# Gradient kernel of an attention layer on one core: o/dQ products of two units together in even units, dK products in odd units

## The chip, the core and the metric

The kernel runs on one core of one Trainium2 chip. The metric is the device time in microseconds (us) of that core; several executions are timed, and a comparison uses executions of both kernels on the same chip. Engines: PE is TensorE (PEld its weight loads), ACT is ScalarE, DVE is VectorE, POOL is GpSimd, SP the engine that issues most DMAs.

## The reference, cut to what matters

The reference computes a linear-attention block (A) and a softmax attention block with 16 query heads and one key/value head (B), and all their gradients. Nearly all the time is in block B, with S = 2048 tokens, 16 heads of 28 channels:

```python
scores = jnp.einsum("bhqd,bkd->bhqk", q, k) * (Dh ** -0.5)
p = _softmax(scores, axis=-1)
o = jnp.einsum("bhqk,bkd->bhqd", p, v)
return (lambda x, *d: x.transpose(*d))(o, 0, 2, 1, 3).reshape(B, S, H * Dh) @ wo
# ... and jax.vjp of all of it with grad_out
```

## The kernel before

The main loop has 512 units. Unit u handles 256 queries, 2 heads and 256 keys; eight units make a block (b = u // 8), after which an accumulator is complete. The forward part of unit u runs beside the backward part of unit w = u - 16. Each unit does, in the program's order:

- "scores": on PE, q.k products into `sps` (two 128x512 tiles, of three buffers) and dO.v products into `dps` (two tiles, of two buffers), contraction over 32 rows: shape 32*128;
- ACT: exp of the first `sps` half (L710), copy of the second `dps` half to `cp` (L717), exp of the second `sps` half (L720);
- DVE: first half of `dsT` = dps times eT (L715); POOL: second half of `dsT` = cp times eT (L718); later DVE transposes dsT into `dsx` (L853);
- PE: dK products (shape 32*32), o, dQ and dV products (shape 128*32).

```python
def mmt(out, lhsT, rhs, pos, start, stop):                       # all these matmuls have line L591
    nc.tensor.matmul(out, lhsT=lhsT, rhs=rhs, start=start, stop=stop, tile_position=pos, ...)

for u in range(NU + 28):                                         # NU = 512
    w = u - 16
    ...
    rows_SD(u, sp, dp)                                           # scores: 4 + 4 matmuls of 256 columns
    ACT:  et[u % 2, 0] = exp(sp[0])                              # L710
    DVE:  dst[0] = dp[0] * ew[0]                                 # L715, dsT of unit w
    ACT:  cp = copy(dp[1])                                       # L717
    POOL: dst[1] = cp * ew[1]                                    # L718
    ACT:  et[u % 2, 1] = exp(sp[1])                              # L720
    ...                                                          # u % 8 == 1: identF transposes of oTs, then rl, onat, don
    ...                                                          # u % 8 == 2: prod; 4: Dq; 6: identB transposes of don -> doT
    x = u - 28                                                   # dK: 3, 3, 3, 3, 2, 2 groups of four matmuls in 6 units of 8
    ...
    v, y = u - 1, u - 18
    for t2 in range(2):                                          # o of unit v, dQ of unit y: 8 matmuls
        ...oq[32*h...]      += vaug . eT[v]
        ...oq[64 + 32*h...] += kn . dsT[y]
    ...                                                          # dV: 8 matmuls of 512 columns in u % 8 == 2 and 3
    ...                                                          # 14 blocks: output projection in a unit u % 8 == 0
    if v % 8 == 7: DVE: oTs = oq[0:64]                           # L844
    if y % 8 == 7: ACT: qT_B = oq[64:128] * scale                # L847, the "dQ copy"
    DVE: dsx[b] = transpose(dsT[y])                              # L853
```

(The block above is abridged and partly paraphrased.)

Of the kernel before, what the change touches and what calls it, by code (L numbers as in the profile page):

```python
# [24 lines left out]
def kernel(  # L25
# [540 lines left out]
    NB = 64  # L566
    NU = NB * 8
# [3 lines left out]
    with ExitStack() as cs_:  # L571
# [16 lines left out]
        eT, eN, dsT, dsx, qX, onat, don, doT, rl, oTs, prod = ({} for _ in range(11))  # L588

        def mmt(out, lhsT, rhs, pos, start, stop):  # L590
            nc.tensor.matmul(out, lhsT=lhsT, rhs=rhs, start=start, stop=stop, tile_position=pos,  # L591
                             skip_group_check=True)

        def blk(b):
            qc, pair = divmod(b, 8)
            return qc, pair, pair // 2, pair % 2
# [91 lines left out]
        with tc.manual_schedule():  # L688
            for u in range(NU + 28):
# [37 lines left out]
                if e >= 0 and e % 8 == 0 and e // 8 < NB:  # L727
                    b = e // 8
# [24 lines left out]
                if e >= 0 and e % 8 == 0 and e // 8 < NB:  # L753
                    b = e // 8
# [9 lines left out]
                if e >= 0 and e % 8 == 0 and e // 8 < NB:  # L764
                    b = e // 8
# [4 lines left out]
                if e >= 0 and e % 8 == 0 and e // 8 < NB:  # L770
                    b = e // 8
# [7 lines left out]
                    doT[b] = pw_.tile([P, 256], BF16, name="doT")  # L779
                    nc.vector.tensor_copy(out=doT[b][r:r + 64, :], in_=tp2[r:r + 64, 0:256])  # L780

                x = u - 28
                if 0 <= x and x // 8 < NB and x % 8 < 6:
                    b = x // 8
                    qc, pair, g, hp = blk(b)
                    m0 = 3 * (x % 8) - max(0, x % 8 - 4)
                    for m in range(m0, m0 + (3 if x % 8 < 4 else 2)):
                        h, B, s = m // 8, (m // 2) % 4, m % 2
                        for a in range(4):
                            rhs = dsx[b][32 * a:32 * a + 32, :, h, :, :].rearrange(  # L790
                                "p u t (b i s) -> p u t b i s", b=4, s=2)[:, :, :, B, :, s]
                            mmt(dk_acc[32 * a:32 * a + 32, :],
                                qX[qc][32 * a:32 * a + 32, B, s, pair * 64 + 32 * h:pair * 64 + 32 * h + 32],
                                rhs, (32 * a, 32 * a), b == 0 and m == 0, b == NB - 1 and m == 15)

                v = u - 1
                y = u - 18
                for t2 in range(2):
                    if 0 <= v < NU:
                        b, tp = divmod(v, 8)  # L800
                        t = 2 * tp + t2
                        for h in range(2):
                            mmt(oq[32 * h:32 * h + 32, 0:256], vaug[:, t, :],
                                eT[v // 2][:, v % 2, h, t2 * 256:(t2 + 1) * 256], (0, 32 * h), t == 0, t == 15)
                    if 0 <= y < NU:
                        b, tp = divmod(y, 8)
                        t = 2 * tp + t2
                        for h in range(2):
                            mmt(oq[64 + 32 * h:96 + 32 * h, 0:256], kn[:, t, :],
                                dsT[y][:, h, t2 * 256:(t2 + 1) * 256], (0, 64 + 32 * h), t == 0, t == 15)  # L810
                if u >= 18 and u % 8 in (2, 3) and (u - 18) // 8 < NB:
                    b, h = divmod(u - 18, 8)
                    for qb in range(2):
                        for c in range(4):
                            rhs = eN[4 * b + c][:, :, :].rearrange("p (u h t q) k -> p u h t q k", u=2, h=2,
                                                                   t=2)[:, :, h, :, qb, :]
                            mmt(dv_acc[32 * c:32 * c + 32, :], don[b][:, qb, h, :], rhs, (0, 32 * c),
                                b == 0 and h + qb == 0, b == NB - 1 and h + qb == 2)
# [20 lines left out]
                if u % 64 in (16, 24) and u > 64:  # L839
                    out_proj(2 * (u // 64 - 1) + u % 64 // 8 - 2)  # L840

                if 0 <= v < NU and v % 8 == 7:
                    oTs[v // 8] = pm_.tile([64, 256], F32, name="oTs")
                    nc.vector.tensor_copy(out=oTs[v // 8][:, :], in_=oq[0:64, 0:256])  # L844
                if 0 <= y < NU and y % 8 == 7:
                    qc, pair, g, hp = blk(y // 8)
                    nc.scalar.activation(out=qT_B[g][64 * hp:64 * hp + 64, qc * 256:(qc + 1) * 256],  # L847
                                         in_=oq[64:128, 0:256], func=ACT.Copy, scale=scale)
                if 0 <= y < NU:
                    b, tp = divmod(y, 8)  # L850
                    if tp == 0:
                        dsx[b] = px_.tile([P, 8, 2, 2, 256], BF16, name="dsx")
                    nc.vector.transpose(  # L853
                        out=dsx[b][:, tp, :, :, :].rearrange("p h t c -> p (h t c)").bitcast(F32),
                        in_=dsT[y][:, :, :].rearrange("p h c -> p (h c)").bitcast(F32))
# [82 lines left out]
```

## Time and profile before

| | before |
|---|---|
| median | 1178.23 us of the first 3 runs; 1176.08 us of 4, with the result |
| length of a usual block of eight units | 12.78 us |
| length of the 14 blocks with an output projection | 13.75 us |

The block lengths, here and below, are worked out from the trace: the distance between the ends of ACT's `cp` (L717) eight units apart; "usual" is the length that most blocks without an output projection share. Pairs of units are measured likewise.

From the page of the kernel before: the span, the busy time of the engines, and costly groups (busy us, mean ns of one | idle time of the engine before them and what ended most of it).

```profile
span 1172.0 us, 38434 instructions
PE 1099.7 (94%) x15388; PEld 444.6 (38%) x15388; DVE 885.5 (76%) x1669; ACT 900.9 (77%) x1788; POOL 699.4 (60%) x835
L718 POOL TENSOR_TENSOR dsT<-cp,eT 128x512 bf16<-128x512 bf16 x512 | 590.3, 1153 | 193.2 <-ACT cp L717 156.2
L710 ACT ACTIVATE eT<-sps 128x512 bf16<-128x512 f32 x512 | 307.3, 600 | 42.2 <-PE dps L591 28.3
L717 ACT ACTIVATE cp<-dps 128x512 bf16<-128x512 f32 x512 | 305.1, 596 | 12.0 <-PE dps L591 11.1
L591 PE MATMUL oq<-dsT,R_65 128*32 128x256 bf16 x2048 | 203.1, 278 | 1.1 <-POOL dsT L718 0.9
```

ACT's three instructions take about 0.60 us each but start 0.48 to 0.49 us apart: 1.46 us a unit. ACT hardly idles. The dQ products do not wait for POOL (0.9 us in all). The waits between 300 and 1100 us say the same (total us, times, longest us):

```profile
ACT eT L710 <- PE dps L591: 24.6, 76, 2.9
ACT R_63 L847 <- PE oq L591: 5.2, 14, 0.4
PE oq L591 <- POOL dsT L718: 0.9, 1, 0.9
```

The timeline of the kernel before (start us, us, instruction):

```profile
603.86 0.28 PE L591 MATMUL sps<-R_63,R_65 32*128 32x256 bf16 x2
604.15 0.83 PE L591 MATMUL dk_acc<-dsx,qX 32*32 32x512 bf16 x12
604.66 0.60 ACT L717 ACTIVATE cp<-dps 128x512 bf16<-128x512 f32 x1
604.91 0.29 PE L591 MATMUL oq<-eT,R_65 128*32 128x256 bf16 x2
605.03 0.28 PE L591 MATMUL oq<-dsT,R_65 128*32 128x256 bf16 x2
605.24 0.28 PE L591 MATMUL sps<-R_63,R_65 32*128 32x256 bf16 x2
605.34 1.15 POOL L718 TENSOR_TENSOR dsT<-cp,eT 128x512 bf16<-128x512 bf16 x1
```

Two things are to be seen. Within a shape the groups of four matmuls start 0.11 us (256 columns) or 0.21 us (512) apart, but a change of shape takes longer: oq at 605.03 to sps at 605.24 is 0.21 us. And the dsT of this unit is finished by POOL at 606.49, 1.25 us after the scores of the next unit have started.

### The profile page before, as it was taken

To read this page: it belongs to the slowest core of one execution; us is meant where nothing else is said; L and a number is where in the kernel's file an instruction comes from. 1 tells how busy PE (TensorE), PEld (TensorE's weight loads), DVE (VectorE), ACT (ScalarE), POOL (GpSimd) and SP (SyncE) were. 2 spreads that over 40 slices of the span, in tenths; PEclk is the share of its full clock that TensorE was granted. 3 is DMA by queue.
4 is the path that set the end of the run, shared out by engine and by line. 5 is a ranking of instruction groups with operands and counts; after the bars stand their busy time and mean duration, and the time that the engine had idled before them with its cause. 6 is when DMAs were issued, how large, how long until landed. Compare 5 with 4: busy or idle time off the path is not lost. (4 is left out here: it accounts for less than half of the span.)

```text
span 1172.0 us, 38434 instructions
## 1 busy us (share of the span) xinstructions
PE 1099.7 (94%) x15388; PEld 444.6 (38%) x15388; DVE 885.5 (76%) x1669; ACT 900.9 (77%) x1788; POOL 699.4 (60%) x835
## 2 busy tenths in 40 slices
PE   7999997988989999999999999999999999999998
PEld 4555543333333333333333333333333333333344
DVE  7886400336889898888889888988999899888922
ACT  3453112357989999999999999999999999999511
POOL 9000150003777777777778777877787778777900
PEclk9999998989999999999999999999999999999999
DMA  9779897059999999999999999999999999999962
GB/s 259 126 130 184 160 188 177 20 125 198 180 179 190 188 164 187 190 184 175 189 188 160 199 188 186 162 198 188 152 195 182 189 170 199 184 168 163 240 147 75
DMA packets 684435, 202.91 MB, mean 173 GB/s; under 512 B 651232, under 2 KB 679392, under 8 KB 684256
## 3 DMA queue, kind: packets, MB, share of 16 engines
q1 hardware_dynamic: 673664, 190.26, 94.8%
q10 hardware_dynamic: 9312, 6.65, 2.1%
q0 software_dynamic: 1280, 3.55, 1.1%
q8 instruction: 120, 1.97, 0.7%
q14 instruction: 59, 0.48, 0.1%
HBM read 22.83 MB, written 15.03 MB: 32 GB/s over the span
## 5 line engine op out<-in xcount | busy, mean ns | idle before, releaser
L718 POOL TENSOR_TENSOR dsT<-cp,eT 128x512 bf16<-128x512 bf16 x512 | 590.3, 1153 | 193.2 <-ACT cp L717 156.2
L715 DVE TENSOR_TENSOR dsT<-dps,eT 128x512 bf16<-128x512 f32 x512 | 347.8, 679 | 58.3 <-PE dps L591 37.6
L853 DVE STREAM_TRANSPOSE dsx<-dsT 128x512 f32<-128x512 f32 x512 | 357.8, 699 | 1.3 <-POOL dsT L718 0.3
L710 ACT ACTIVATE eT<-sps 128x512 bf16<-128x512 f32 x512 | 307.3, 600 | 42.2 <-PE dps L591 28.3
L591 PEld LDWEIGHTS <-R_65 32*128 32x128 bf16 (+1 forms) x8192 | 171.5, 92 | 403.3 <-issue 356.1
L717 ACT ACTIVATE cp<-dps 128x512 bf16<-128x512 f32 x512 | 305.1, 596 | 12.0 <-PE dps L591 11.1
L720 ACT ACTIVATE eT<-sps 128x512 bf16<-128x512 f32 x512 | 311.6, 609 | 0.0
L591 PE MATMUL dk_acc<-dsx,qX 32*32 32x512 bf16 x4096 | 290.4, 377 | 0.0
L591 PE MATMUL dps<-doT,R_65 32*128 32x256 bf16 x2048 | 253.9, 271 | 7.7 <-DVE R_64 L824 1.1
L591 PE MATMUL sps<-R_63,R_65 32*128 32x256 bf16 x2048 | 242.9, 276 | 5.9 <-ACT eT L710 2.0
L591 PE MATMUL oq<-eT,R_65 128*32 128x256 bf16 x2048 | 213.8, 278 | 2.5 <-issue 0.3
L591 PE MATMUL oq<-dsT,R_65 128*32 128x256 bf16 x2048 | 203.1, 278 | 1.1 <-POOL dsT L718 0.9
L591 PEld LDWEIGHTS <-qX 32*32 32x32 bf16 x4096 | 69.4, 89 | 94.1 <-issue 54.1
L591 PE MATMUL dv_acc<-eN,don 128*32 128x512 bf16 x1024 | 86.9, 382 | 2.5 <-DMA eN<-eT 2.5
L521 DVE TENSOR_TENSOR osb<-R_65 32x512 bf16<-32x512 bf16 x4 | 1.7, 413 | 74.2 <-ACT R_65 L518 74.2
L380 POOL MEMSET ga<- 64x448 bf16 x2 | 0.9, 468 | 90.8 <-PE agen L337 71.3
L553 POOL MEMSET R_65<- 128x16 bf16 x1 | 0.2, 172 | 70.8 <-DVE R_65 L552 70.8
L748 POOL TENSOR_TENSOR don<-R_64,rl 128x128 bf16<-128x128 bf16 x64 | 25.8, 403 | 21.4 <-DVE rl L740 21.4
L844 DVE COPY oTs<-oq 64x256 f32<-64x256 f32 x64 | 26.5, 414 | 15.1 <-PE oq L591 14.4
L731 PE MATMUL sps<-identF,oTs 64*128 64x64 f32 x128 | 21.3, 247 | 17.0 <-DVE oTs L844 10.6
L591 PEld LDWEIGHTS <-don 128*32 128x32 bf16 x1024 | 34.7, 97 | 4.0 <-issue 3.9
L79 PEld LDWEIGHTS <-R_64 128*128 128x128 bf16 x256 | 23.9, 100 | 28.0 <-issue 10.3
(216 smaller groups left out, 961.2 us busy)
## 6 DMA issues: line engine op xcount, KB each, us to landing
qX<-qn_d SPq DMA_DIRECT2D x128, 64.0 KB
out_dram<-osb ACTq DMA_DIRECT2D x44, 112.0 KB
eN<-eT SPq DMA_TRANSPOSE x256
qn_d<-dsx SPq DMA_DIRECT2D x1, 2048.0 KB
on_d<-onat SPq DMA_DIRECT2D x8, 256.0 KB
xa<-in_A_x_dram SPq DMA_DIRECT2D x8, 224.0 KB
ga<-in_grad_out_dram SPq DMA_DIRECT2D x4, 448.0 KB
xa<-in_grad_out_dram POOLq DMA_DIRECT2D x4, 448.0 KB, 4.7
```

Source lines behind the costliest of these rows:

```text
L79: nc.tensor.matmul(out_ap, lhsT=lhsT, rhs=rhs, start=start, stop=stop, tile_position=(0, 0))
L521: nc.vector.tensor_tensor(out=sq[0:32, :], in0=kT[0:32, qc * 512:(qc + 1) * 512], in1=kT[0:32, qc * 512:(qc + 1) * 512], op=ALU.mult)
L591: nc.tensor.matmul(out, lhsT=lhsT, rhs=rhs, start=start, stop=stop, tile_position=pos, skip_group_check=True)
L710: nc.scalar.activation(out=et[:, u % 2, 0, :], in_=sp[0][:, :], func=ACT.Exp, scale=scale)
L715: nc.vector.tensor_tensor(out=dst[:, 0, :], in0=dp[0][:, :], in1=ew[:, w % 2, 0, :], op=ALU.mult)
L717: nc.scalar.activation(out=cp[:, :], in_=dp[1][:, :], func=ACT.Copy)
L718: nc.gpsimd.tensor_tensor(out=dst[:, 1, :], in0=cp[:, :], in1=ew[:, w % 2, 1, :], op=ALU.mult)
L720: nc.scalar.activation(out=et[:, u % 2, 1, :], in_=sp[1][:, :], func=ACT.Exp, scale=scale)
L731: nc.tensor.transpose(onp[:, qb, :, :].rearrange("p h c -> p (h c)"), oTs[b][0:64, qb * P:(qb + 1) * P], identF[0:64, 0:64], tile_position ...
L748: nc.gpsimd.tensor_tensor(out=dn[:], in0=dnv, in1=r_[:].to_broadcast([P, 2, 2, 32]), op=ALU.mult)
L844: nc.vector.tensor_copy(out=oTs[v // 8][:, :], in_=oq[0:64, 0:256])
L853: nc.vector.transpose(out=dsx[b][:, tp, :, :, :].rearrange("p h t c -> p (h t c)").bitcast(F32), in_=dsT[y][:, :, :].rearrange("p h c -> p ...
```

## The change

The intent is fewer changes of tile shape on PE: scores then dK in odd units, scores then o/dQ/dV of two units in even ones, 16 changes a block instead of 22. No work is added or removed.

```diff
-                x = u - 28
-                if 0 <= x and x // 8 < NB and x % 8 < 6:
+                x = u - 27
+                if 0 <= x and x // 8 < NB and x % 2 == 0:
                     b = x // 8
-                    m0 = 3 * (x % 8) - max(0, x % 8 - 4)
-                    for m in range(m0, m0 + (3 if x % 8 < 4 else 2)):
+                    for m in range(4 * (x % 8 // 2), 4 * (x % 8 // 2) + 4):
 ...
-                v = u - 1
-                y = u - 18
-                for t2 in range(2):
+                v, y = u - 1, u - 17
+                for d in range(4 if u % 2 == 0 else 0):
+                    t2 = d % 2
+                    v_, y_ = v - 1 + d // 2, y - 1 + d // 2
 ...   (o of units v_, dQ of units y_: eT[v_], dsT[y_])
-                if u >= 18 and u % 8 in (2, 3) and (u - 18) // 8 < NB:
+                if u >= 18 and u % 8 in (2, 4) and (u - 18) // 8 < NB:
 ...
-                if 0 <= v < NU and v % 8 == 7:
+                if u % 2 == 0 and 0 <= v < NU and v % 8 == 7:
 ...   (oTs copy on DVE)
-                if 0 <= y < NU and y % 8 == 7:
+                if u % 2 == 0 and 0 <= y < NU and y % 8 == 7:
 ...   (dQ copy on ACT; y is now u - 17, so this falls in the unit of the oTs copy)
+                y = u - 18
```

More of the change, by code (lines that the diff above doesn't have):

```diff
@@ L794 @@
                                 rhs, (32 * a, 32 * a), b == 0 and m == 0, b == NB - 1 and m == 15)
-                v = u - 1
-                y = u - 18
-                for t2 in range(2):
-                    if 0 <= v < NU:
-                        b, tp = divmod(v, 8)
-                        t = 2 * tp + t2
+                v, y = u - 1, u - 17
+                for d in range(4 if u % 2 == 0 else 0):
+                    t2 = d % 2
+                    v_, y_ = v - 1 + d // 2, y - 1 + d // 2
+                    if 0 <= v_ < NU:
+                        t = 2 * (v_ % 8) + t2
                         for h in range(2):
                             mmt(oq[32 * h:32 * h + 32, 0:256], vaug[:, t, :],
-                                eT[v // 2][:, v % 2, h, t2 * 256:(t2 + 1) * 256], (0, 32 * h), t == 0, t == 15)
-                    if 0 <= y < NU:
-                        b, tp = divmod(y, 8)
-                        t = 2 * tp + t2
+                                eT[v_ // 2][:, v_ % 2, h, t2 * 256:(t2 + 1) * 256], (0, 32 * h), t == 0, t == 15)
+                    if 0 <= y_ < NU:
+                        t = 2 * (y_ % 8) + t2
                         for h in range(2):
                             mmt(oq[64 + 32 * h:96 + 32 * h, 0:256], kn[:, t, :],
-                                dsT[y][:, h, t2 * 256:(t2 + 1) * 256], (0, 64 + 32 * h), t == 0, t == 15)
-                if u >= 18 and u % 8 in (2, 3) and (u - 18) // 8 < NB:
-                    b, h = divmod(u - 18, 8)
+                                dsT[y_][:, h, t2 * 256:(t2 + 1) * 256], (0, 64 + 32 * h), t == 0, t == 15)
+                if u >= 18 and u % 8 in (2, 4) and (u - 18) // 8 < NB:
+                    b, h = (u - 18) // 8, (u - 18) % 8 // 2
                     for qb in range(2):
```

## The prediction

> **What bounds it now.** The 512 main units run from about 248 to 1114 us. In the windows view (300 to 1100 us) TensorE is busy about 95%, ScalarE about 95%, VectorE 89%, GpSimd 77%. The timeline shows a repeating block of eight units of 12.78 us (13.75 where the output projection falls in; 14 of 64 blocks). ScalarE's three 512-column instructions of a unit start 0.49, 0.48 and 0.49 us apart when nothing delays them: 1.46 us a unit, and with the dQ copy about 12.05 us a block. So ScalarE is nearly the floor; the other 0.7 us are waits for late scores (waits view: ScalarE eT and cp on dps, 29 us between 300 and 1100). TensorE's score products stretch from 0.13 to 0.47 us in the units where it is ahead, because they need the dP buffer that cp frees.
>
> **What the change does.** It removes changes of tile shape on TensorE: 22 a block become 16. In the timeline, last start to first start is 195 ns from scores to the next shape (about 110 within a shape), 301 from dK to o/dQ (213 within), 205 from o/dQ to scores: 90 to 100 ns a change. The Trainium skill, "TensorEngine Tiling (Array Packing)", Overview, Key Properties, says a mode change drains TensorE; the trace agrees, with these 90 to 100 ns. Saved: about 0.6 us of TensorE a block, 11.1 to 10.5 us. No work is added.
>
> The danger: in even units dQ now reads the dsT of the unit just before (lag 17 instead of 18). Its second half is made by GpSimd in 1.15 us, starting 0.08 us after cp ends. In the trace GpSimd's product of an odd unit ends 0.9 to 1.5 us after the next unit's score products start; the new dQ matmuls want it about 0.55 us after. TensorE is in order ("TensorE: Matmul & The Clock Gate", Part 3: matmuls are strict FIFO), so dV and the next scores wait behind it.
>
> That makes a loop over two units, from the end of cp(odd) to the end of the next cp(odd): GpSimd 1.23, semaphore 0.06, last dQ round 0.11, change to scores 0.21, scores to first exp 0.42, exp to cp 0.49, cp 0.60: 3.12 us, against ScalarE's 2.92 for two units. Where dV follows in the even unit (two pairs of four), 0.43 more: 3.54. In the pair with the dQ copy ScalarE sets about 3.33. Sum 3.33 + 3.54 + 3.54 + 3.12 = 13.53 us a block, +0.75 against 12.78, times 64 = +48 us. The blocks with an output projection win back about 0.3 us each, 4 to 5 us; start and end nearly unchanged.
>
> **Predicted: 1219 us**, range 1194 to 1240. Faster by over 2%: 0.09; within 2%: 0.17; slower: 0.74.
>
> **What would show it right.** A new wait of TensorE's oq matmuls on GpSimd's dsT, about 0.7 us in most even units, some 100 to 170 us in all; ScalarE's eT waits on dps/sps growing to over 60 us, mostly before odd units; block about 13.5 us; changes of shape still 90 to 100 ns each.
>
> **What would make it wrong.** If the released o/dQ wait is shorter than I think (scores of even units starting later relative to cp, so that GpSimd is done), only the saved changes count: the block would fall to ScalarE's 12.1 to 12.4 us, 25 to 40 us faster. If GpSimd falls behind through its small don/prod products, it is slower still.

## The result, and the profile after

The change measured 1245.63 us (1244.65 to 1247.84, 4 runs) against 1176.08 us. The ratio is 1.0595 with a 95% interval of 1.056 to 1.063. Ratios here are the mean time of one kernel's runs over that of the other's of the same rounds, so not quite the ratio of the quoted medians. The direction was as predicted, but the loss was 70 us, not 43.

The same parts of the page after (L843 is the oTs copy, L846 the dQ copy), with the line of the chain of waits (a chain followed back from the last instruction of the program):

```profile
span 1244.3 us, 38379 instructions
PE 1094.4 (88%) x15379; PEld 462.3 (37%) x15388; DVE 887.7 (71%) x1669; ACT 917.0 (74%) x1788; POOL 702.0 (56%) x835
PE 38%; POOL 22%; issue 18%; ACT 12%; DVE 6%; DMA 2%; SPq 1%; POOLq 0%; ACTq 0%; DVEq 0%
L718 POOL TENSOR_TENSOR dsT<-cp,eT 128x512 bf16<-128x512 bf16 x512 | 590.4, 1153 | 265.2 <-ACT cp L717 235.2
L710 ACT ACTIVATE eT<-sps 128x512 bf16<-128x512 f32 x512 | 305.7, 597 | 69.9 <-PE dps L591 53.0
L591 PE MATMUL oq<-dsT,R 128*32 128x256 bf16 x2048 | 226.0, 277 | 76.8 <-POOL dsT L718 74.7
L846 ACT ACTIVATE R<-oq 64x256 bf16<-64x256 f32 x64 | 24.3, 379 | 36.3 <-DVE oTs L843 34.5
```

No instruction became slower: L718 still takes 1153 ns and L710 597. What is new is waiting. The dQ products wait for POOL, the exp waits for late scores (69.9 us of idle before it instead of 42.2), and the small dQ copy has 36.3 us of idle before it, most of it ended by DVE's oTs copy. POOL, an engine at 56%, makes up 22% of the chain of waits. (The page of the kernel before follows its chain over the last 5% of the span only, so there is no share to compare this with.)

The first timeline of the change is one turn of a loop over two units, here in a pair with dV:

```profile
641.49 0.59 ACT L717 ACTIVATE cp<-dps 128x512 bf16<-128x512 f32 x1
642.15 1.15 POOL L718 TENSOR_TENSOR dsT<-cp,eT 128x512 bf16<-128x512 bf16 x1 [0.38 <-ACT cp L717]
642.67 0.27 PE L591 MATMUL oq<-dsT,R 128*32 128x256 bf16 x1
643.36 0.27 PE L591 MATMUL oq<-dsT,R 128*32 128x256 bf16 x1 [0.42 <-POOL dsT L718]
643.48 0.69 PE L591 MATMUL dv_acc<-eN,don 128*32 128x512 bf16 x8
644.10 0.28 PE L591 MATMUL sps<-R,R 32*128 32x256 bf16 x2
644.53 0.60 ACT L710 ACTIVATE eT<-sps 128x512 bf16<-128x512 f32 x1 [0.45 <-PE dps L591]
645.02 0.59 ACT L717 ACTIVATE cp<-dps 128x512 bf16<-128x512 f32 x1
```

Read it as a ring: cp ends (642.08), POOL makes its half of dsT (until 643.30), the dQ product that needs it goes at 643.36, dV behind it, then the next scores, the exp, and the next cp of the same parity, which ends at 645.61. That is 3.53 us for two units, and ACT alone would need 2.92. The dQ product started 0.69 us after the one before it (642.67 to 643.36), where 0.11 us is usual; the bracket says 0.42 because a matmul's own 0.27 us counts as busy. The Trainium skill, "Perfetto Trace Analysis", Tensor Engine Instruction, says that a matmul's reported end is computed, not observed; here that makes the profile's sum of 74.7 us too small a measure of the wait.

The second timeline is the unit with both copies out of the accumulator:

```profile
648.12 0.59 ACT L717 ACTIVATE cp<-dps 128x512 bf16<-128x512 f32 x1
650.01 0.37 PE L591 MATMUL oq<-dsT,R 128*32 128x256 bf16 x2
650.11 0.60 ACT L720 ACTIVATE eT<-sps 128x512 bf16<-128x512 f32 x1
650.31 0.28 PE L591 MATMUL sps<-R,R 32*128 32x256 bf16 x2
650.48 0.42 DVE L843 COPY oTs<-oq 64x256 f32<-64x256 f32 x1 [0.66 <-PE oq L591]
650.93 0.38 ACT L846 ACTIVATE R<-oq 64x256 bf16<-64x256 f32 x1 [0.22 <-DVE oTs L843]
651.34 0.60 ACT L710 ACTIVATE eT<-sps 128x512 bf16<-128x512 f32 x1
651.83 0.59 ACT L717 ACTIVATE cp<-dps 128x512 bf16<-128x512 f32 x1
```

The accumulator is complete at about 650.4, and ACT is busy with its exp until 650.71. The dQ copy does not start then but at 650.93, when DVE's copy has ended, and the next exp, whose scores were started at 650.31, starts only after it. This pair takes 3.71 us from cp to cp. In the prediction it had 3.33. The wait for DVE is 0.22 us of it; what the rest is, e3 shows below.

The periods by pair of units (from the end of cp of one odd unit to the next, u % 8 given, usual blocks) set the prediction beside the result:

| pair | before | predicted | after |
|---|---|---|---|
| 7 to 1 (dQ copy) | 2.98 | 3.33 | 3.71 |
| 1 to 3 (dV) | 3.48 | 3.54 | 3.54 |
| 3 to 5 (dV) | 2.98 | 3.54 | 3.53 |
| 5 to 7 | 3.34 | 3.12 | 3.10 |
| sum | 12.78 | 13.53 | 13.88 |

(The pair labels are of the kernel after; before, the dQ copy was in pair 1 to 3 and dV in units 2 and 3.) The blocks with an output projection rose from 13.75 to 15.27 us. The trace has 63 block lengths: 49 times 1.10 us and 14 times 1.52 us make 75 us, and the stretch from the first cp to the last rose by 75 us (833 to 908 us).

### The profile page after: what moved, and what is told of

It reads as the page before. It is cut to its first block, busy times and chain, and to the rows that moved or that the text cites. A ratio compares the mean times of both kernels' runs of the same rounds, so it can differ in the third digit from the quotient of the medians.

```text
span 1244.3 us, 38379 instructions
## 1 busy us (share of the span) xinstructions
PE 1094.4 (88%) x15379; PEld 462.3 (37%) x15388; DVE 887.7 (71%) x1669; ACT 917.0 (74%) x1788; POOL 702.0 (56%) x835
## 4 chain that ended last, share of the span: by engine, by line
PE 38%; POOL 22%; issue 18%; ACT 12%; DVE 6%; DMA 2%; SPq 1%; POOLq 0%; ACTq 0%; DVEq 0%
POOL dsT L718 19%; PE agen L79 10%; PE dk_acc L591 8%; ACT cp L717 6%; PE oq L591 5%; ACT eT L720 4%; PE sps L79 4%; PE sps L591 3%; PE aacc L79 3%; PE dv_acc L591 2%; POOL prod L757 2%; DVE oTs L843 2%; PE dps L79 2%; PE sps L731 1%; DVE dsT L715 1%
## 5 line engine op out<-in xcount | busy, mean ns | idle before, releaser
L718 POOL TENSOR_TENSOR dsT<-cp,eT 128x512 bf16<-128x512 bf16 x512 | 590.4, 1153 | 265.2 <-ACT cp L717 235.2
L715 DVE TENSOR_TENSOR dsT<-dps,eT 128x512 bf16<-128x512 f32 x512 | 348.6, 681 | 109.4 <-PE dps L591 77.6
L710 ACT ACTIVATE eT<-sps 128x512 bf16<-128x512 f32 x512 | 305.7, 597 | 69.9 <-PE dps L591 53.0
L591 PEld LDWEIGHTS <-R 32*128 32x128 bf16 (+1 forms) x8192 | 179.9, 93 | 441.3 <-issue 413.0
L591 PE MATMUL oq<-dsT,R 128*32 128x256 bf16 x2048 | 226.0, 277 | 76.8 <-POOL dsT L718 74.7
L591 PE MATMUL dk_acc<-dsx,qX 32*32 32x512 bf16 x4096 | 268.5, 376 | 0.0
L591 PE MATMUL sps<-R,R 32*128 32x256 bf16 x2048 | 248.0, 277 | 8.4 <-ACT eT L710 4.1
L591 PE MATMUL dps<-doT,R 32*128 32x256 bf16 x2048 | 244.0, 274 | 1.5 <-DVE R L823 1.1
L591 PE MATMUL oq<-eT,R 128*32 128x256 bf16 x2048 | 202.2, 280 | 0.0
L591 PEld LDWEIGHTS <-qX 32*32 32x32 bf16 x4096 | 79.8, 89 | 107.1 <-issue 42.7
L846 ACT ACTIVATE R<-oq 64x256 bf16<-64x256 f32 x64 | 24.3, 379 | 36.3 <-DVE oTs L843 34.5
L843 DVE COPY oTs<-oq 64x256 f32<-64x256 f32 x64 | 26.5, 414 | 32.1 <-PE oq L591 31.1
L79 PEld LDWEIGHTS <-R 128*128 128x128 bf16 (+1 forms) x416 | 34.1, 99 | 35.7 <-issue 11.4
```

Source lines behind the costliest of these rows:

```text
L79: nc.tensor.matmul(out_ap, lhsT=lhsT, rhs=rhs, start=start, stop=stop, tile_position=(0, 0))
L710: nc.scalar.activation(out=et[:, u % 2, 0, :], in_=sp[0][:, :], func=ACT.Exp, scale=scale)
L715: nc.vector.tensor_tensor(out=dst[:, 0, :], in0=dp[0][:, :], in1=ew[:, w % 2, 0, :], op=ALU.mult)
L718: nc.gpsimd.tensor_tensor(out=dst[:, 1, :], in0=cp[:, :], in1=ew[:, w % 2, 1, :], op=ALU.mult)
L843: nc.vector.tensor_copy(out=oTs[v // 8][:, :], in_=oq[0:64, 0:256])
L846: nc.scalar.activation(out=qT_B[g][64 * hp:64 * hp + 64, qc * 256:(qc + 1) * 256], in_=oq[64:128, 0:256], func=ACT.Copy, scale=scale)
```

## The experiments

The theory is: (1) the dQ products of the newest dsT wait for POOL and close a loop over two units; (2) what the prediction lacked is in the pair with the dQ copy, which is queued behind the oTs copy. The rival to (1) is that bursts of two units' products by themselves make the scores late. All twelve runs gave correct outputs.

| run | usual block | block with projection | time (median) | ratio to before, 95% |
|---|---|---|---|---|
| before | 12.78 | 13.75 | 1176.08 | |
| the change | 13.88 | 15.27 | 1245.63 | 1.060 (1.056 to 1.063) |
| e1_lag19 | 12.95 | 13.64 | 1181.46 | 1.004 (1.000 to 1.008) |
| e2_copy_odd | 13.33 | 14.58 | 1213.4 | 1.031 (1.027 to 1.035) |
| e3_copy_first | 13.91 | 14.57 | 1246.25 | 1.059 (1.055 to 1.063) |
| e4_dv_first | 13.11 | 14.43 | 1200.42 | 1.019 (1.015 to 1.023) |
| e5_dk_only | 13.83 | 14.37 | 1229.52 | 1.047 (1.045 to 1.049) |
| e6_oq_only | 14.41 | 15.80 | 1326.71 | 1.130 (1.125 to 1.135) |
| e7_lag19_idt2 | 12.62 | 13.66 | 1166.9 | 0.993 (0.991 to 0.995) |
| e8_dv_copy | 12.90 | 14.15 | 1188.42 | 1.011 (1.009 to 1.013) |
| e9_prod10 | 12.45 | 13.48 | 1163.81 | 0.988 (0.985 to 0.992) |
| e10_split_out | 12.45 | 12.94 (28 blocks) | 1165.26 | 0.990 (0.986 to 0.993) |
| e11_cast_last | 13.88 | 14.25 | 1235.19 | 1.050 (1.046 to 1.054) |
| e12_before_split | 12.78 | 13.27 (28 blocks) | 1176.74 | 1.001 (0.997 to 1.005) |

### e1: dQ two units later

```diff
-                v, y = u - 1, u - 17
+                v, y = u - 1, u - 19
-  cdsT bufs=4, ceN bufs=11          (one more dsT buffer; one fewer eN buffer, to make room)
+  cdsT bufs=5, ceN bufs=10
-                if u == 530:        (a later load of dQ, moved to where it is complete)
+                if u == 532:
```

> The change with one thing different: the dQ pair of an even unit reads the dsT of the units 20 and 19 back instead of 18 and 17 (one more dsT buffer, one fewer eN buffer to make room). Main theory (the slowdown is TensorE's wait for the GpSimd half of the newest dsT): that wait goes to about nothing, the block falls from 13.88 us to about 12.4 to 12.7, time 1140 to 1170 us. Rival (the bursts of a two-unit o/dQ product and a four-group dK product by themselves make the scores late, whatever dsT is read): the time stays above 1200 us.

The wait on POOL is gone. The group of the same products, in the view of groups for e1:

```profile
L591 PE MATMUL oq<-dsT,R 128*32 128x256 bf16 x2048 | 159.5, 278 | 0.0
```

The time fell to 1181.46 us, 64 us less than the change. So most of the loss was the lag, and the rival, taken as the whole, is refuted. (e1 also has one dsT buffer more. In the change neither instruction that writes dsT, L715 or L718, has a wait that a dQ product ended, by their --source views, so a lack of dsT buffers was not what e1 removed.) But the time missed the expectation of 1140 to 1170 us: the block is 12.95 us, still longer than before. Three pairs of four now run at 2.98 us, ACT's own pace; the pair 1 to 3 takes 4.02. That is one place, and e7 looks there.

### e2 and e3: the two copies

```diff
 e2:
-                if u % 2 == 0 and 0 <= y < NU and y % 8 == 7:      (y = u - 17: unit u % 8 == 0)
+                y = u - 18
+                if 0 <= y < NU and y % 8 == 7:                     (unit u % 8 == 1)
 e3: the two copies in the other order in the program, ACT's dQ copy first
```

> The change, with ScalarE's dQ copy moved back to the odd unit after (as late as before the change), so that it isn't behind VectorE's oTs copy in the same unit. Theory (the part that the prediction lacked, 26 us, is that this copy waits 0.38 us for the oTs copy in the two units where it falls, and holds back the next exp): the pair of units with the copy falls from 3.71 to about 3.1 to 3.3 us, the block to 13.3 to 13.5, time 1208 to 1222 us. Rival (the copy fits in idle time of ScalarE and the missing part is elsewhere): 1240 to 1250 us.

> The change, with the two copies out of the accumulator oq in the other order in the program: ScalarE's dQ copy first, VectorE's oTs copy second. Theory A (the two readers of one accumulator are made to follow each other in program order): ScalarE no longer waits for oTs, but oTs now waits for ScalarE's copy and the transposes after it come later; time within 1% of the change, 1235 to 1257 us. Theory B (only ScalarE's copy is held, nothing holds oTs): 1218 to 1226 us.

In e2 the pair 7 to 1 fell from 3.71 to 3.10 us and the time by 32 us, as expected: in the odd unit ACT does the copy while it would be waiting for the loop anyway (pair 1 to 3 stayed at 3.54). In e3 the time stayed, 1246.25 us, and the wait changed sides. From the waits of e3, 300 to 1100 us:

```profile
DVE oTs L847 <- ACT R L843: 57.2, 43, 1.6
```

So the two readers of one accumulator follow each other in the order in which the program has them, although one reads its rows 0 to 63 and the other 64 to 127. In the instructions of both traces the second copy waits on a semaphore that the first updates. Whether they could overlap was not tried; taking that wait alone away was not an option.

e3 shows one thing more: how long the pair is when the dQ copy waits for nothing, as the prediction had it. From the timeline of e3:

```profile
655.04 0.60 ACT L720 ACTIVATE eT<-sps 128x512 bf16<-128x512 f32 x1
655.67 0.38 ACT L843 ACTIVATE R<-oq 64x256 bf16<-64x256 f32 x1
656.07 0.60 ACT L710 ACTIVATE eT<-sps 128x512 bf16<-128x512 f32 x1
656.08 0.42 DVE L847 COPY oTs<-oq 64x256 f32<-64x256 f32 x1 [1.32 <-ACT R L843]
```

ACT is never idle for more than 0.03 us in this pair, and still it takes 3.51 us, not 3.33: the copy of 0.38 us starts 0.03 us after the exp before it has ended and is followed by a gap of 0.02 us, while the large instructions overlap, so that the two exps start 1.03 us apart instead of 0.49. The kernel before has the same in its pair with the copy (3.48 us, no idle of ACT over 0.04 us). So of the 0.38 us that the prediction missed in this pair, about 0.18 is ACT's own time with the copy and about 0.20 the wait for oTs. The expectation of e2 put all of it down to the wait. That the time of e3 stayed is a balance: its pairs 1 to 3 and 3 to 5 grew, by 0.13 and 0.10 us, as oTs and what follows from it came later.

### e4 and e8: dV before the newest dQ

```diff
 e4, in an even unit:
-   o(u-2), dQ(u-18), o(u-1), dQ(u-17), dV
+   o(u-2), dQ(u-18), o(u-1), dV, dQ(u-17)
 e8: e4 and e2 together
```

> The change, with only the order of TensorE within an even unit different: both units' o products, the older dQ product and the dV products first, the dQ product that reads the newest dsT last. Theory (a loop over two units goes cp, GpSimd product, last dQ products, then dV, then the scores of the next unit): dV (0.43 us) leaves the loop in two pairs of four, their period falls from 3.53 to about 3.1 us, the block from 13.88 to about 13.0, time about 1191 us (1183 to 1200). Rival (length of TensorE's bursts): nothing changes, 1240 to 1250 us.

> Both repairs together at the change's own lag: dV before the newest dQ (as e4) and the dQ copy in the odd unit (as e2). Theory: all four pairs of a block then run at the loop of 3.1 us through cp, GpSimd, dQ, scores, exp: block about 12.5 us, 1155 to 1168 us, faster than before although TensorE still waits on GpSimd in every even unit. If the two repairs did not add up, 1180 to 1200 us.

In e4 nothing but the order on PE inside one unit differs, and 45 us go: the two dV pairs fall from 3.54 and 3.53 us to 3.11 and 3.18. The time, 1200.42 us, lies at the upper edge of what was expected (1183 to 1200). This is the strongest support for the loop: dV's 0.43 us counts where it stands behind the awaited product and counts nothing where it fills the wait. The length of PE's burst is the same in both.

e8 missed: 1188.42 us instead of 1155 to 1168. Its pairs are 3.10, 3.48, 3.20 and 3.11 us. The repairs do not add up because e2's copy had been hidden in the wait that e4 removes: with dV out of the loop, pair 1 to 3 is bound by ACT with the copy, 3.48 us, as in the kernel before (no idle of ACT over 0.04 us in either). The expectation had all four pairs at 3.1 us and left this out.

### e5 and e6: the two halves of the change alone

```diff
 e5: the kernel before, with the dK part of the change only (x = u - 27, four groups in each odd unit)
 e6: the change, with dK as in the kernel before (x = u - 28, six units of eight)
```

> The kernel before with the dK part of the change alone: dK in four odd units of four groups, o, dQ and dV as before in every unit (20 changes of tile shape a block instead of 22). Theory (what counts is when the longest unit on TensorE exceeds the about 1.5 us that ScalarE gives it): an odd unit becomes scores 0.33, dK 0.97, o/dQ 0.34 = 1.64 us, with dV 2.07, with the transposes 2.1, so the block is about 13.8 us and the time about 1235 us (1215 to 1255). Rival (fewer changes of shape are worth their time, whatever unit they fall in): 1168 to 1174 us.

> The change with its dK part undone: o, dQ and dV in even units for two units, dQ reading the newest dsT, but dK spread over six units as before. Now dK stands between the scores and the o/dQ products of even units, so TensorE asks for the newest dsT about 0.5 to 0.8 us later and its wait on GpSimd should shrink to under half; but those units are longer. Theory: block about 14.2 us, 1255 to 1275 us. If the wait on GpSimd were the whole story, and not the length of the even unit up to the next scores: well under 1220 us.

e5 came out as expected in the block, 13.83 us, and at 1229.52 us in time. It has no wait of dQ on POOL and two changes of shape fewer than before, and loses 55 us, because its odd units exceed the about 1.5 us that ACT needs for a unit: from cp to cp it takes 1.75 to 2.26 us after an odd unit and 1.47, ACT's own pace, after an even one, so nothing is won back. So bursts do cost when a unit is too long: in that sense the rival is a real effect, but not what made the change slow.

e6 is the worst, 1326.71 us against an expected 1255 to 1275. The wait on POOL shrank as expected (16.4 us between 300 and 1100 us, against 65.3), and the usual block is 14.41 us (expected 14.2). The rest is a lower granted clock: its mean is 0.934, and in the stretch from 656 to 660 us, in a block with an output projection, it is 0.50. In the trace 20 blocks of the main loop have such a stretch of 6.8 us in them, with and without a projection; they take 16.8 to 18.3 us, about 2.5 us more than others of their kind, and no block without one is longer than 15.80. That is about 50 us. Single stretches at 0.50 are in the main loop of other runs too (e3, e9 and e10, three or four each, most of 3.4 us); the kernel before and the change have none from 302 us to the end of the loop. Why the clock fell, and so much more often here, is open.

### e7 and e9: what e1 still lost

```diff
 e7, on e1: the identF transposes and what follows from them one unit later
-                e = u - 9          (transposes of oTs, rl, onat, don)
+                e = u - 10
-                e = u - 10         (prod on POOL)
+                e = u - 11
-                if u % 64 == 1 and u > 1:    (load of the finished o)
+                if u % 64 == 2 and u > 2:
 e9: as e7, but prod at u - 10 again
```

> The run with dQ two units later (e1), with the transposes of o and what follows from them one unit later, so that they are in an even unit and no longer beside sixteen dK products. Theory for the rest of e1 (12.95 us a block): in the odd unit with the transposes TensorE is too long by 0.5 us, and ScalarE's exp waits; moved to the even unit before ScalarE's dQ copy the delay is hidden behind that copy. Block about 12.45 us, 1140 to 1160 us, faster than the kernel before. Rival (e1's rest is a general cost of bursts): 1175 to 1185 us.

> As e7, but with GpSimd's product behind VectorE's small sum (prod) back in the unit where it was before, just after the transposes' results. In e7 that product ran one unit later and VectorE waited for it, 33 us in all, and the scores three units on were 0.17 us late. Theory: that part goes, the block falls from 12.62 to about 12.45 us, the time to 1152 to 1160 us. If the sum's wait was not what made them late: 1164 to 1168 us as e7.

In e1 the odd unit 1 holds the transposes and sixteen dK products. With the transposes moved to unit 2, e7's pair 1 to 3 fell from 4.02 to 3.52 us, and its time to 1166.9 us, a little below the kernel before. It fell less than expected (12.62 us a block, not 12.45, and 1140 to 1160 us), and the waits of e7 (300 to 1080 us) show why: a POOL product that was moved along held up DVE.

```profile
DVE Dq L767 <- POOL prod L757: 33.2, 61, 0.6
```

e9 puts it back behind the transposes' results. That wait no longer appears, and the usual block is 12.45 us, as first expected of e7. The time is 1163.81 us, ratio 0.988 (0.985 to 0.992): faster than the kernel before by 1.2%, clear of the noise but within 2%, and the median is a few us above the range expected (1152 to 1160; its runs scatter from 1159 to 1168). Its block is three pairs of 2.98 us and one of 3.52 with the dQ copy, and in that one ACT has no idle over 0.03 us: ACT's own time, which the prediction had as 12.05 us a block.

### e10, e11 and e12: the output projection

```diff
 e10, on e9, and e12, on the kernel before: a tile's projection in two halves of 224 columns, in two blocks
-                if u % 64 in (16, 24) and u > 64:
+                if u % 64 in (16, 24, 32, 40) and 64 < u < 512:    (28 blocks)
 e11, on the change: out_proj(...) after the two copies out of oq in the program
```

> e9, with the output projection of a tile cut into two halves of 224 columns in two different even units (28 blocks with a half, instead of 14 with a whole). Theory (a unit of TensorE over about 1.5 us delays ScalarE by the excess, a shorter one by nothing): the even unit with a whole is 0.88 + 0.86 = 1.74 us and more, with a half about 1.5, so the about 1.0 us that 14 blocks lose shrinks to under 0.3 us in 28; time 1140 to 1152 us. Rival (the work itself costs its time wherever it is): no gain, or a loss of up to 5 us, as four more matmuls a tile are issued.

> The change, with the output projection put after the two copies out of oq in the program, so that VectorE copies oTs before it copies the projection out. TensorE's order stays. Theory (the second missing term: in 14 blocks oTs waits behind that copy on VectorE, ScalarE's dQ copy waits for oTs, and the next exp for that): these blocks fall from 15.27 to 14.2 to 14.5 us, time 1230 to 1237 us. Rival (those blocks are long because of TensorE's work alone): 1243 to 1248 us.

> Control for e10: the kernel before with the same cut of the output projection into halves. Theory: the 0.97 us that 14 blocks lose there shrinks too, but TensorE has less room in each unit (1.42 us against 0.88 us in an even unit of the alternating form), so a part of it stays: 1166 to 1174 us. If the cut is worth as much here as in e10, the alternation has no part in that gain.

e11 confirms the second missing term. In the change the 14 blocks cost 1.39 us more than a usual one; with DVE copying oTs before the projection they cost 0.37 us more (14.25 against 13.88), and 10 us of time go.

e10 failed: 28 blocks lose 0.49 us each instead of 14 losing 1.03, and the time is as e9's. e12 does the same to the kernel before with the same outcome. The reason is in e10's timeline:

```profile
618.96 0.56 PE L79 MATMUL sps<-wo,oTq 128*128 128x224 bf16 x4
619.44 0.60 ACT L720 ACTIVATE eT<-sps 128x512 bf16<-128x512 f32 x1
620.10 0.26 PE L591 MATMUL sps<-R,R 32*128 32x256 bf16 x1 [0.37 <-ACT eT L720]
620.43 0.60 ACT L710 ACTIVATE eT<-sps 128x512 bf16<-128x512 f32 x1 [0.39 <-PE sps L591]
```

The projection takes one of the three `sps` buffers. The next unit's second score product must then wait for the second exp of the unit before (it ends at 620.04) instead of the first, and ACT waits in turn. All 28 blocks of e10 have this wait, and the pair 7 to 1 is 3.47 us instead of 2.98 in e9, e10 and e12 alike, whether the projection is whole or half. A whole one in e9 costs another 0.54 us in the pair 1 to 3, which the half does not: there the expectation held. It had counted only PE's length, and left the buffer out. (A fourth buffer was not tried.) e12 missed its range too, 1176.74 us instead of 1166 to 1174.

## Why the prediction was right or wrong

- **ACT as the floor, PE and ACT taking turns:** right in the pairs without the dQ copy. With POOL out of the loop (e1, e9) they run at 2.98 us, 0.06 above the 2.92 of the prediction. With the copy ACT needs 3.48 to 3.52 us, so a block in which it waits for nothing is 12.45 us (e9), not 12.05.
- **Changes of shape cost about 90 to 100 ns, six fewer a block:** right, and without effect in the change. There the same distances are 195 to 198 (scores to the next shape), 303 to 305 (dK to scores) and 203 ns (dQ to scores). The Trainium skill, "TensorEngine Tiling (Array Packing)", Key Properties (in its section on the modes, not in the Overview), says that a change of tiling mode drains TensorE; the extra distance fits that, though a drain as such is not to be seen in a trace. The 0.6 us of PE that they free are not in the loop; no run here takes them alone.
- **The loop through cp, GpSimd, last dQ, dV, scores, exp:** right, to 0.02 us: 3.12 and 3.54 us predicted, 3.10, 3.53 and 3.54 measured, shown by e1 (lag) and e4 (order). It is not luck: its terms, too, are those of the ring above to about 0.02 us. The Trainium skill, "TensorE: Matmul & The Clock Gate", Part 3, says that matmuls start and end in order; that is why dV and the scores stood behind one product, and e4 agrees: with dV before that product the dV pairs are 0.43 and 0.35 us shorter.
- **Wrong: "In the pair with the dQ copy ScalarE sets about 3.33."** The pair measured 3.71 us, and two things were wrong. ACT's own time with the copy was mis-sized: where the copy waits for nothing, the pair takes 3.51 us (e3), and 3.48 could be read from the kernel before. And the prediction let the copy start when ACT was free; it waited 0.22 us for DVE's oTs copy, which had been in another unit before the change and is in the same unit now. With 0.38 us a block over 64 blocks this is 24 us, about half from each; moving the copy (e2) took away 32 us.
- **Wrong: "The blocks with an output projection win back about 0.3 us each."** They lost 0.42 us more each than before (1.39 us over a usual block, against 0.97), as oTs stood behind the projection's copy on DVE too. Against the prediction this is 0.72 us in 14 blocks, 10 us. e11 shows it: with oTs first they cost 0.37 us over a usual block, so 0.60 would have been won back.
- **Together** these two terms are 34 us; the other three pairs were 0.03 us a block shorter than predicted, 2 us in all. The trace's loss between first and last cp is 75 us, and 43 predicted plus 34 less 2 is 75. In the timed medians the loss is 70 us; the first cp came about 3 us earlier in the profiled run of the change, and the rest is within the scatter of runs.
- **The signs named:** by the starts, the dQ products wait 0.58 to 0.70 us in about three of four even units and 0.30 in the others. From start to start these are 148 us over the run, within the "100 to 170 us" named; the profile's own sum, 74.7 us, is below it, because a matmul's modelled length runs into the wait. ACT's exp waited 63 us for scores (`dps` 53.0, `sps` 10.4), as predicted ("over 60"), mostly before odd units. The block was 13.88, not 13.5.

## What to carry to other kernels

When work of two steps is gathered into one, first list which results each gathered product now reads earlier: one unit of lag less closed a loop through the slowest producer, and that cost far more than the saved mode changes were worth. Inside such a loop only what stands behind the awaited instruction counts, so independent work belongs before it; and small copies that move into the same unit can queue behind each other on different engines, and can cost their own engine more than they last (0.54 us for a copy of 0.38 in e3), where a sum of durations doesn't see them. When ACT sets the pace, every unit has to fit its time by itself (short units don't pay for long ones), and each repair has to be measured with the others, since one may have been hidden in the wait that another removes.

## What the Trainium skill lacked or had wrong

- "TensorEngine Tiling (Array Packing)", Key Properties, says that a mode change drains TensorE but gives no cost. Here it is about 90 to 100 ns: last start to first start 195 to 198 ns from 256-column scores and 301 to 305 ns from 512-column dK products, against about 110 and 213 ns inside a shape.
- "PSUM — Partial Sum Buffer", PSUM bank collisions raise a hardware error, says that accesses of two engines to different quadrants of one bank run clean. The two readers of oq here use different quadrants (rows 0 to 63 and 64 to 127), and the compiled program makes them wait for each other all the same, in program order: 34.5 us of idle before the dQ copy in the whole run of the change, 63.6 us before the oTs copy in that of e3. The page doesn't warn of such a wait. That the accesses could overlap is not shown by any run here.
- "ScalarE: Activation LUTs", What ACT_TABLE_LOAD costs, gives an overlap of about 93 ns of back-to-back ACTIVATEs. Here instructions of 512 columns overlap by 0.07 to 0.12 us, which fits; but around the dQ copy (64x256) there is no overlap, and gaps of 0.02 to 0.04 us instead (kernel before, e3, e9). The page doesn't say when the overlap is missing, and no run here shows why.
- No page that was read tells that a sum of waits before matmuls in a profile is short by the modelled length of the matmul before: 0.69 us from start to start appear as 0.42 us here.
- The granted clock of e6 fell to 0.50 in stretches in which PE still had work (3.5 of 4 us busy, by the profile, from 656 to 660 us). "TensorE: Matmul & The Clock Gate", Part 1, ties the half clock to an idle window of about 3.4 us; the longest idle stretch of TensorE's matmuls in e6's trace between 648 and 660 us is 0.71 us. The same part also tells of a kernel in which frequent short idles between groups of matmuls made the clock swing, without saying how much idle is enough; whether that is the case here was not settled.
